# Order, engines and filler products listed anew, from the first loads to the first late expert, in a kernel of attention and four experts

## The chip, the cores and the metric

The kernel runs on one core of a Trainium2 chip. The metric is device time in microseconds (us) for one execution, lower being better. Before the change it is 454.83 us, the median of three runs (452.33 to 455.21).

A core has engines with a queue of instructions each: PE (TensorE, matrix products), DVE (VectorE), ACT (ScalarE), POOL (GpSimd), and SP, which here only issues loads and stores. They wait for each other by semaphores. Every engine takes its own instructions strictly in the order in which they were written.

## The reference

```python
def _attn_ref(q, k, v):                      # B, H, S, D = 2, 8, 576, 64
    q_d, k_d, v_d = (mean over groups of 4 positions of q, k, v)
    out_d  = softmax(q_d @ k_d.T / 8) @ v_d  # 144 x 144 for each head
    out_up = np.repeat(out_d, 4, axis=2)
    mask = np.abs(pos[:, None] - pos[None, :]) < 4
    out_local = softmax(where(mask, q @ k.T / 8, -1e9)) @ v
    return out_up + out_local

def _moe_ref(x, domain_probs, w1, w2):       # x 1152 x 512, 4 experts, w1 512 x 1024, w2 1024 x 512
    p = domain_probs / (domain_probs.sum(-1, keepdims=True) + 1e-09)
    for e in range(4):
        out += p[:, e:e + 1] * (np.maximum(x @ w1[e], 0.0) @ w2[e])
    return out
```

The tokens x of the second function are the output of the first, 2 batches by 576 positions, 8 heads by 64 side by side. All inputs and the output are float32.

## The kernel before

**Stages.** Attention is done in four parts, `a0` to `a3`: two batches by two halves of 288 positions. Expert 0 runs between them in blocks of tokens `m00` to `m03` (256, 256, 256 and 384 tokens), as soon as the parts that make those tokens are through. The late experts 1 to 3 follow, each as sums of tokens and weights (`x1` to `x4`, `s`, `t`, `w`) and products `p110`, `p510` and so on (L1033), then second products `s110` ... (L1222, L1235). Before them `a0` alone has only small work for PE.

**Steps of an attention part**, by the last part of their names, with the line that issues them:

- loads (SP): `q0n`, `k00n`, `k01n`, `v00n`, `v01n` in halves of four heads (L244); `a1q.0` to `.3` and `k10r`, `k11r` by rows (L255); `vw` windows of v (L276); `raw100` ... `raw201` weights of expert 0 (L290); `praw` the probabilities.
- rows: `q0r`, `k00r`, `k01r` copy the loaded heads into another order (L189 on ScalarE, L191 on VectorE). `k00t`, `qt` are transposes on PE (L340), four to a step, `k00te`, `qte` the copies back (L183 to L191).
- pooled path, 144 columns: `qds`, `k00ds` and `k01ds` sum rows (L375, L376), `qdt`, `k00dt`, `k01dt` transpose them (L381), `qde`, `k00de` copy them; in later parts `qd` and `k10d` reduce instead (L359). `ds` products (L675), `dm` maximum (L689), `de` exponential (L697), `da`, `db` sum and reciprocal (L707, L709), `dq` share (L714), `dt` transpose (L722), `dc` copy, `dv` product with the summed values `v00d`, `v01d` (L745), `xd` copy. These come in four groups, 0 to 3; of `ds` and `dv` two groups go in one piece, with the later of the two names.
- local path, three tiles of 96 positions, 0 to 2: `sc0.0` and `sc0.1` are the products of a tile's scores for four heads each (L522), in `a0` with two products that add the mask (L512); `madd` (L545), `max` (L556, L560), `sub` (L567, L571), `exp` (L574), `sum`, `eps`, `rec` (L578 to L586), `norm` (L589), `blk` (32x32 transposes on VectorE, L593), `pv` product with the window (L602).
- `xs` adds both paths (L615), `xh` is its rounded copy and `xl` the remainder (L626).

**Steps of expert 0.** `whi` is a weight's rounded copy (L189 on ScalarE) and `wlo` its remainder (L306, 128x1024; POOL does it in four pieces, VectorE in one). `m00.m0` to `.m7` are the first products of block m00, 12 matmuls each (L778), `r` and `l` their rectified high and low parts (L785 and L789), `m00.o00` ... the second products in four parts to a tile of 128 tokens (L803), `g` the weighted result (L810).

**What sets the order.** Nothing is planned when the program is built. Every piece of work is a named step with a default engine; a table `ENGINE` overrides the engine of some (V, G or A), and a table `ORDER` lists all 1320 names:

```python
def step(name, eng, deps, fn):
    steps[name] = (ENGINE.get(name, eng), deps, fn)
...
for name in order(steps):          # order() returns ORDER
    steps[name][2]()
```

So each engine's queue holds its steps in the order of the table. A step that must wait holds up everything behind it on the same engine. A third table, `WARM`, gives 46 counts: step `warm7` puts `WARM[7]` products of a 64x64 tile of zeros on PE, whose result nobody reads.

```python
for _ in range(n):
    nc.tensor.matmul(T["wps"][:64, :64], wz, wz, start=True, stop=True)
```

**Buffers that tie steps.** Small products share a pool of three PSUM tiles and the larger ones another pool of three (`ps_g`, `ps_m`). The rows of `a2q` go where those of `k11r` were, so its load waits for the four transposes `k11t`; `a1q` goes where `q0r` was.

Of the kernel before, what the change touches and what calls it, by code (L numbers as in the profile page):

```python
# [1381 lines left out]
```

## Time and profile before

| | us |
|---|---|
| median of three runs | 454.83 (452.33 to 455.21) |
| the profiled execution, its own time | 456.84 |
| its span | 455.1 |

| engine | busy in the span | instructions |
|---|---|---|
| PE, products | 443.3 us (97%) | 4266 |
| PE, weight loads | 420.6 us (92%) | 4266 |
| DVE | 337.8 us (74%) | 592 |
| ACT | 208.3 us (46%) | 391 |
| POOL | 104.7 us (23%) | 126 |

The profile is one execution. The span goes from its first to its last instruction; the profiled execution's time is 1.7 us longer. The mean granted clock of PE over the span is 0.977 of full speed. TensorE's clock has two levels, 1.2 and 2.4 GHz; a granted clock of 0.50 is the lower and 1.00 the upper. A float32 product appears as two records on PE, so six 64x64 products are a group of x12.

In a chain of waits a row says from when on, and how long, an engine or a DMA held up the work that ended last. A row of the view of lines gives minimum, median and maximum duration in ns. Where a row of a timeline ends in brackets, they hold the engine's idle time just before it and what ended that.

### The profile page before, as it was taken

To read this page: it belongs to the slowest core of one execution; us is meant where nothing else is said; L and a number is where in the kernel's file an instruction comes from. 1 tells how busy PE (TensorE), PEld (TensorE's weight loads), DVE (VectorE), ACT (ScalarE), POOL (GpSimd) and SP (SyncE) were. 2 spreads that over 40 slices of the span, in tenths; PEclk is the share of its full clock that TensorE was granted. 3 is DMA by queue.
4 is the path that set the end of the run, shared out by engine and by line. 5 is a ranking of instruction groups with operands and counts; after the bars stand their busy time and mean duration, and the time that the engine had idled before them with its cause. 6 is when DMAs were issued, how large, how long until landed. Compare 5 with 4: busy or idle time off the path is not lost.

```text
span 455.1 us, 10197 instructions
## 1 busy us (share of the span) xinstructions
PE 443.3 (97%) x4266; PEld 420.6 (92%) x4266; DVE 337.8 (74%) x592; ACT 208.3 (46%) x391; POOL 104.7 (23%) x126
## 2 busy tenths in 40 slices
PE   8998798999999999999999999999999999999996
PEld 7777687898897998999999999999999999999996
DVE  4669778678678898556579985666799846678983
ACT  4666542332141433554466517444664164446630
POOL 5559941140011000121332121012321100013020
PEclk9758999999999999999999999999999999999999
DMA  7889424501101030662466494334655923135135
GB/s 172 218 196 241 102 58 108 105 18 34 37 1 48 2 93 1 169 109 81 83 118 91 112 168 94 46 101 88 104 80 130 185 58 46 48 62 94 31 94 163
DMA packets 69086, 43.11 MB, mean 95 GB/s; under 512 B 27632, under 2 KB 66992, under 8 KB 69040
## 3 DMA queue, kind: packets, MB, share of 16 engines
q1 hardware_dynamic: 55392, 30.14, 25.4%
q0 software_dynamic: 13648, 12.32, 18.4%
q8 instruction: 33, 0.54, 0.5%
q14 instruction: 13, 0.11, 0.1%
HBM read 36.69 MB, written 2.36 MB: 86 GB/s over the span
## 4 chain that ended last, share of the span: by engine, by line
PE 87%; POOL 4%; DMA 4%; DVE 2%; SPq 1%; issue 1%; ACT 1%; POOLq 0%; ACTq 0%
PE ps L1033 29%; PE ps L1222 26%; PE ps L1235 4%; PE m03h L778 4%; PE m03o L803 4%; POOL wlo L306 3%; PE m02h L778 3%; PE m01h L778 3%; PE m01o L803 3%; PE m02o L803 2%; PE m00o L803 2%; PE m00h L778 1%; DMA acc<-in_q_dram 1%; DMA vw<-in_v_dram 1%; DMA q0n<-in_q_dram 1%; SPq L276 1%
## 5 line engine op out<-in xcount | busy, mean ns | idle before, releaser
L1222 PE MATMUL ps<-slot,unit 128*128 128x256 f32 x1008 | 119.7, 280 | 0.0
L1222 PEld LDWEIGHTS ps<-slot,unit 128*128 128x128 f32 x1008 | 119.0, 189 | 0.0
L1033 PE MATMUL ps<-xhi,slot 128*128 128x288 f32 x384 | 66.5, 295 | 0.0
L1033 PE MATMUL ps<-xc,slot 128*128 128x288 f32 x432 | 59.8, 295 | 0.0
L1033 PEld LDWEIGHTS ps<-xc,slot 128*128 128x128 f32 x432 | 58.2, 188 | 0.0
L1033 PEld LDWEIGHTS ps<-xhi,slot 128*128 128x128 f32 x384 | 56.3, 188 | 0.1
L1045 ACT ACTIVATE H<-ps 128x288 f32<-128x288 f32 x72 | 27.8, 411 | 50.1 <-PE ps L1033 50.0
L1082 POOL DMA_DIRECT2D raw<-in_moe_w_dram x15 | 19.5, 1297 | 133.4 <-DVE slot L1088 74.7
L987 DVE TENSOR_TENSOR slot<-raw,slot 128x1792 fp32r<-128x1792 f32 x12 | 24.3, 2022 | 26.7 <-PE ps L1033 24.3
L1049 DVE TENSOR_TENSOR H<-H,ps 128x288 f32<-128x288 f32 x72 | 29.3, 449 | 19.6 <-PE ps L1033 19.6
L189 ACT CAST slot<-raw 128x1024 fp32r<-128x1024 f32 (+1 forms) x33 | 41.8, 1279 | 2.8 <-DVE raw L981 2.0
L1033 PE MATMUL ps<-xlo,slot 128*128 128x288 f32 x192 | 41.1, 295 | 0.0
L1133 ACT ACTIVATE unit<-H 128x512 fp32r<-128x512 f32 (+1 forms) x24 | 20.0, 844 | 28.6 <-DVE H L1049 18.2
L1137 ACT ACTIVATE unit<-H 128x1024 fp32r<-128x1024 f32 x18 | 19.1, 1062 | 29.1 <-PE ps L1222 19.2
L1033 PEld LDWEIGHTS ps<-xlo,slot 128*128 128x128 f32 x192 | 30.7, 188 | 0.0
L1120 DVE SCALAR_TENSOR_TENSOR H<-H 128x1024 f32<-128x1024 f32 (+1 forms) x18 | 28.1, 1574 | 1.9 <-ACT H L1047 1.6
L1146 DVE SCALAR_TENSOR_TENSOR unit<-H,unit 128x1024 fp32r<-128x1024 f32 x18 | 22.0, 1222 | 8.1 <-ACT unit L1137 8.0
L1088 DVE TENSOR_TENSOR slot<-raw,slot 128x1024 fp32r<-128x1024 f32 x21 | 25.3, 1218 | 2.4 <-ACT slot L189 2.4
L1142 DVE SCALAR_TENSOR_TENSOR unit<-H,unit 128x512 fp32r<-128x512 f32 (+1 forms) x24 | 22.5, 954 | 3.0 <-ACT unit L1133 3.0
L1244 DVE SCALAR_TENSOR_TENSOR acc<-ps,npr,acc 128x256 f32<-128x256 f32 x48 | 20.7, 476 | 2.9 <-PE ps L1222 2.9
L306 POOL TENSOR_TENSOR wlo<-raw,whi 128x256 fp32r<-128x256 f32 x28 | 21.7, 805 | 1.2 <-ACT whi L189 1.1
L975 POOL DMA_DIRECT2D raw<-in_moe_w_dram x8 | 11.8, 1469 | 41.0 <-DMA raw<-in_moe_w_dram 23.2
(328 smaller groups left out, 775.8 us busy)
## 6 DMA issues: line engine op xcount, KB each, us to landing
raw<-in_moe_w_dram POOLq DMA_DIRECT2D x15, 512.0 KB, 6.1
raw<-in_moe_w_dram SPq DMA_DIRECT2D x24, 256.0 KB
raw<-in_moe_w_dram SPq DMA_DIRECT2D x12, 512.0 KB
...
```

What stands on the lines that cost most here:

```text
L189: nc.scalar.copy(out_, in_)
L306: eng.tensor_tensor(a[:, us], b[:, us], c[:, us], ALU.subtract)
L778: nc.tensor.matmul(ps[:, :n], w[:, d, cc:cc + P], x[:, d, n0:n0 + n], start=i == 0, stop=i == len(terms) - 1,)
L803: nc.tensor.matmul(ps[:, cs], T[f"{nm}t{f}"][:, hpart, cc:cc + P], w[:, f % 4, cs], start=f == 0 and x == 0, stop=f == KF - 1 and x == 2,)
L987: engine(f"wo{e}{i}").tensor_tensor(w1tile(i, 1), raw1(e, i), f32(w1tile(i, 0)), ALU.subtract)
L1033: nc.tensor.matmul(bank(acc_, n, i)[:, :NH // 2], w[:, d * P:(d + 1) * P], x[:, d, n * (NH // 2):(n + 1) * (NH // 2)], start=u == 0 and fi ...
L1045: nc.scalar.mul(dst, at, -1.0)
L1049: nc.vector.tensor_tensor(dst, dst, at, ALU.add)
L1088: engine(f"bo{e}{m}").tensor_tensor(w2tile(m, 1), raw2(q), f32(w2tile(m, 0)), ALU.subtract)
L1120: nc.vector.scalar_tensor_tensor(at[o], at[x], 0.0, at[y], ALU.max, op)
L1142: nc.vector.scalar_tensor_tensor(o, x, 0.0, y, ALU.max, ALU.subtract)
L1222: nc.tensor.matmul(ps[:, t * 256:t * 256 + 256], a[:, f, t * P:t * P + P], b[:, f], start=first_ and (t, f, x) == (0, 0, 0), stop=(t, f, x ...
```

## The change

Only the three tables are written anew. No function changes, no step is added or removed, and the numbers computed are the same.

`WARM` goes from 69 products to 86. Steps that carry none or few may now stand elsewhere, too.

```diff
-WARM = [14, 0, 0, 0, 0, 0, 0, 0, 0, 0, 0, 0, 0, 1, 0, 0, 1, 0, 0, 0, 0, 3, 0, 0, 0, 0, 1, 3, 2, 0, 0, 0, 0, 0, 2, 0, 1, 3, 0, 0, 14, 6, 6, 3, 3, 6]
+WARM = [12, 0, 0, 0, 2, 0, 0, 3, 2, 0, 2, 0, 2, 1, 0, 0, 2, 0, 0, 0, 0, 6, 0, 0, 0, 0, 0, 2, 0, 3, 1, 0, 0, 0, 2, 0, 0, 3, 2, 0, 14, 6, 6, 3, 9, 3]
```

`ENGINE` differs in 43 entries. To VectorE go `q0r.0`, `k00te.0`, `k01r.1`, `a0.dc2`, `a0.xh0`, `a1.dc1`, `a1.dc2`, `a1.xh0`, `k11te.0`, `k11te.3`, `whi201.1`, `a2.qte.0`, `a3.qte.0`, `a3.xh2` from ScalarE and `v01d.1`, `v10d.1`, `a1.norm0`, `a1.sub2`, `a1.dq0`, `a2.xl0`, `a3.xl2` from POOL. To POOL go `k00ds.1`, `k01ds.0`, `v11d.0`, `a0.norm2`, `a1.norm1`, `a2.norm0`, `a2.sub0`, `a2.dq2`, `a2.xl1`, `a3.norm1`, `a3.sub0`, `a3.dq0`, `a3.dq2` and to ScalarE `k10te.3`, `a1.xh1`, `a2.dc0`, all from VectorE. A few more entries repeat a default or name a load, and move nothing.

`ORDER` differs up to about the first expert's second products; from `s110` on PE has the rows it had. The loads on SP stand in another order: before, `k01n`, `v00n`, `v01n.1`, `raw100`, `v01n.0`, the four of `a1q`, `vw01`, `raw101`; after, `v01n.0` ahead of `k01n`, then `v00n.0`, `v01n.1`, `vw01`, `a1q.1`, `v00n.1`, `a1q.2`, `raw100`, `a1q.0`, `vw00`, `a1q.3`, `raw101`, `raw200`. Two lines of it, around the first scores:

```diff
-    k00te.1 k00te.0 a0.qte.0 warm4 k00t.2 warm19 a0.qte.2 a0.qte.1 k00t.3 k00te.3 k00te.2 a0.qte.3 a0.sc0.0 a0.sc0.1
+    a0.qte.0 k00te.1 v00d.1 k00t.2 warm19 vw00 a0.qte.3 a1q.3 a0.qte.1 a0.qte.2 a0.sc0.0 k00te.2 warm5 k00t.3 warm4
```

In the rows that follow, the names behind a line number are result and operands, with the number of the buffer; `wps` is the unread result of the warm products.

PE before, from the transposes of the pooled q (`a_qdt`) to the first tile's scores (`a0sl` from keys `kT` and queries `a0qT`):

```order
L381 MATMUL a_qdt<-ident,a0.qdp 128x72 x4
L232 MATMUL wps<-wz 64x64 x6
L340 MATMUL k00t_184<-ident,acc 128x72 x4
L340 MATMUL k00t_189<-ident,acc 128x72 x4
L232 MATMUL wps<-wz 64x64 x6
...
L232 MATMUL wps<-wz 64x64
L340 MATMUL k00t_279<-ident,acc 128x72 x4
L340 MATMUL k00t_286<-ident,acc 128x72 x4
L512 MATMUL a0sl<-mask,ident 128x128 x2
L522 MATMUL a0sl<-kT_121,a0qT 32x32 x32
L381 MATMUL k00dt<-ident,k00dp 128x72 x4
```

PE now, at the same place:

```order
L381 MATMUL a_qdt<-ident,a0.qdp 128x72 x4
L232 MATMUL wps<-wz 64x64 x9
L340 MATMUL k00t_185<-ident,acc 128x72 x4
L232 MATMUL wps<-wz 64x64 x2
...
L340 MATMUL k00t_284<-ident,acc 128x72 x4
L512 MATMUL a0sl<-mask,ident 128x128 x2
L522 MATMUL a0sl<-kT_240,a0qT 32x32 x16
L340 MATMUL k00t_319<-ident,acc 128x72 x4
L232 MATMUL wps<-wz 64x64 x3
L381 MATMUL k01dt<-ident,k01dp 128x72 x4
L232 MATMUL wps<-wz 64x64 x2
L522 MATMUL a0sl<-kT_240,a0qT 32x32 x16
```

The scores of the first tile were one row of 32 and are now two of 16; the last key transposes, warm products and `k01dt` stand between them, and more warm products stand ahead.

PE before, behind the first group of value products `a0po` and ahead of `a0.pv0` (`a0pv`):

```order
L722 MATMUL a0pdt_568<-ident,a0pd_507 72x72 x4
L722 MATMUL a0pdt_578<-ident,a0pd_529 72x72 x4
L232 MATMUL wps<-wz 64x64 x3
L602 MATMUL a0pv_588<-ptb_92,vw_334 64x96 x8
L745 MATMUL a0po<-a0pts_573,vd_265 64x72
```

PE now:

```order
L722 MATMUL a0pdt_576<-ident,a0pd_523 72x72 x4
L722 MATMUL a0pdt_590<-ident,a0pd_537 72x72 x4
L232 MATMUL wps<-wz 64x64 x11
L602 MATMUL a0pv_608<-ptb_92,vw_289 64x96 x8
L745 MATMUL a0po<-a0pts_584,vd_268 64x72
```

Eleven warm products stand there instead of three.

VectorE before, in part a1, from the remainder `wlo200.1` (L306) to two of m00's low parts (L789):

```order
L306 TENSOR_TENSOR wlo_815<-raw_650,whi_693 128x1024
L789 SCALAR_TENSOR_TENSOR m00t_843<-m00h_773,m00t_843 128x256
...
L191 COPY a1pts_899<-a1pdt_891 72x288
L707 TENSOR_SCALAR a1dsm<-a1dsm 72x2
L560 TENSOR_REDUCE a1mx_927<-a1pm_846 128x8
L789 SCALAR_TENSOR_TENSOR m00t_854<-m00h_792,m00t_854 128x256
L689 TENSOR_REDUCE a1dmx<-a1sd_834 72x2
```

VectorE now:

```order
L306 TENSOR_TENSOR wlo_834<-raw_617,whi_709 128x1024
...
L191 CAST whi_827<-raw_672 128x1024
L714 TENSOR_TENSOR a1pd_829<-a1pd_829,a1dsm 72x288
...
L191 COPY a1pts_914<-a1pdt_906 72x288
L560 TENSOR_REDUCE a1mx_919<-a1pm_832 128x8
L789 SCALAR_TENSOR_TENSOR m00t_889<-m00h_809,m00t_889 128x256
L560 TENSOR_REDUCE a1mx_944<-a1pm_882 128x8
L707 TENSOR_SCALAR a1dsm<-a1dsm 72x2
```

The step `m00.l3` (the second L789 before, `m00t_889` now) stood behind `a1.da2` (L707) and now stands ahead of it. The cast `whi201.1` and the share `a1.dq0` (L714) have come in ahead of the copy `a1.dc0` (`a1pts`).

## Rows read from the trace of the kernel before

**Rows 1.** The page: busy time and instructions by engine; the chain's shares by engine.

```profile
PE 443.3 (97%) x4266; PEld 420.6 (92%) x4266; DVE 337.8 (74%) x592; ACT 208.3 (46%) x391; POOL 104.7 (23%) x126
...
PE 87%; POOL 4%; DMA 4%; DVE 2%; SPq 1%; issue 1%; ACT 1%; POOLq 0%; ACTq 0%
```

**Rows 2.** Stretches: start:end, length, busy by engine (instructions), PEclk, DMA share, GB/s.

```profile
9.60:16.50 6.90, 6.18 (x102) 5.17 (x104) 6.24 (x15) 4.81 (x9) 1.47 (x3) 1.00 0.96 234
16.50:37.00 20.50, 20.23 (x297) 16.71 (x298) 12.72 (x46) 11.68 (x32) 14.46 (x20) 0.50 0.85 215
37.00:43.00 6.00, 5.26 (x186) 4.55 (x187) 5.61 (x12) 3.94 (x7) 5.98 (x9) 1.00 1.03 266
43.00:79.50 36.50, 32.26 (x372) 27.69 (x359) 29.18 (x72) 16.61 (x44) 19.16 (x30) 1.00 0.42 90
79.50:182.20 102.70, 102.52 (x1103) 90.16 (x1104) 84.35 (x173) 34.19 (x84) 12.85 (x17) 1.00 0.16 38
```

**Rows 3.** The chain that ended last: start, length, engine, result, line.

```profile
79.50 0.95 PE a_qt L340 x12
...
182.28 44.57 PE ps L1033 x336
```

**Rows 4.** Waits of PE from 0 to 190 us: total, times, longest.

```profile
PE m00h L778 <- DVE m00t L789: 1.3, 1, 1.3
...
PE a1pdt L722 <- POOL a1pd L714: 1.2, 1, 1.2
...
PE a_qt L340 <- DMA acc<-in_q_dram: 0.3, 1, 0.3
```

**Rows 5.** Timeline of PE, 9.5 to 44 us: start, length, operation.

```profile
9.53 0.91 PE L232 MATMUL wps<-wz 128*64 128x64 f32 x12
...
15.59 0.36 PE L522 MATMUL a0sl<-kT,a0qT 64*32 64x32 f32 x32
...
16.99 0.36 PE L522 MATMUL a0sl<-kT,a0qT 64*32 64x32 f32 x16 [0.15 <-ACT a0qT L183]
...
22.38 1.59 PE L675 MATMUL a0sd<-kd,a0qd 64*72 64x144 f32 x8
...
28.77 1.33 PE L232 MATMUL wps<-wz 128*64 128x64 f32 x10
30.03 0.70 PE L722 MATMUL a0pdt<-ident,a0pd 72*72 72x72 f32 x4
...
35.69 1.31 PE L745 MATMUL a0po<-a0pts,vd 72*64 72x72 f32 x16
```

**Rows 6.** Timeline of PE behind 45 us, the same kind of product as at 22.38.

```profile
45.59 0.71 PE L675 MATMUL a1sd<-kd,a1qd 64*72 64x144 f32 x8
```

**Rows 7.** Timeline of VectorE, 37 to 46 us.

```profile
37.48 0.56 DVE L615 TENSOR_TENSOR a0x<-a0pv,a0xd 128x384 f32<-128x384 f32 x1 [0.21 <-ACT a0xd L189]
37.96 1.77 DVE L593 STREAM_TRANSPOSE ptb<-a0pm 32x256 f32<-32x256 f32 x4
...
42.24 0.41 DVE L191 CAST xhi<-a0x 128x384 fp32r<-128x384 f32 x1
...
44.24 0.54 DVE L626 TENSOR_TENSOR xlo<-a0x,xhi 128x384 fp32r<-128x384 f32 x1
44.71 0.74 DVE L359 TENSOR_REDUCE a1qd<-a1qT 128x144 f32<-128x576 f32 x1
```

**Rows 8.** Durations of single lines: ns minimum/median/maximum, first and last start.

```profile
L714 DVE TENSOR_TENSOR a1pd<-a1pd,a1dsm x1: 445/445/445, 57.7 to 57.7; 72x288 f32<-72x288 f32 x1
...
L707 DVE TENSOR_SCALAR a0dsm<-a0dsm x4: 165/166/475, 25.4 to 31.7; 72x2 f32<-72x2 f32 x4
L707 DVE TENSOR_SCALAR a1dsm<-a1dsm x4: 456/592/1360, 47.7 to 56.7; 72x2 f32<-72x2 f32 x4
...
L189 ACT CAST whi<-raw x8: 1035/1042/1051, 31.8 to 49.5; 128x1024 fp32r<-128x1024 f32 x8
...
L189 ACT COPY kT<-k01t x3: 673/673/710, 22.0 to 26.7; 128x288 f32<-128x288 f32 x3
```

More of the change, by code (lines that the diff above doesn't have):

```diff
@@ L31 @@
-    a0.sum0 a0.db1 a0.ds2 a0.ds3 a0.dm2 a0.dm3 k01te.3 warm9 a0.sc2.1 warm35 warm38 a0.dq0 a0.dt0 a0.dc0 a0.eps0
-    a0.dq1 a0.rec0 a0.max2 a0.de2 a0.sub2 warm28 warm27 a0.dt1 a0.norm0 a0.da2 a0.dc1 a0.db2 a0.dq2 a0.de3 a0.da3
-    a0.eps1 a0.db3 a0.blk0.1 a0.rec1 a0.exp2 a0.blk0.0 a0.sum2 a0.dq3 a0.norm1 whi100.1 wlo100.1 a0.eps2 a0.blk1.1
-    a0.rec2 a0.blk1.0 warm26 a0.dv1 a0.dv0 a0.dt2 a0.dc2 a0.norm2 whi101.0 a0.dt3 a0.dv2 warm8 a0.dc3 warm44 a0.pv0
-    a0.dv3 a1.qt.1 whi100.0 a0.xd a0.xs0 a1.qt.3 warm45 a0.pv1 a1.qt.2 a0.blk2.0 a0.blk2.1 vw02 k10r.3 raw200 k10r.2
@@ new lines @@
+    a0.rec0 a0.dc0 a0.de2 warm28 a0.sub2 warm27 a0.dt1 a0.da2 a0.de3 a0.db2 a0.dc1 a0.dq2 a0.exp2 a0.da3 a0.eps1
+    a0.norm0 a0.rec1 a0.db3 a0.blk0.1 a0.dq3 a0.sum2 a0.blk0.0 a0.norm1 whi100.1 a0.eps2 warm1 wlo100.1 a0.rec2 a0.dv1
+    warm26 a0.dv0 a0.dt2 a0.norm2 whi101.0 a0.dc2 a0.blk1.1 a0.blk1.0 a0.dt3 warm8 a0.dc3 warm44 a0.dv2 a0.pv0 raw200
+    a0.dv3 a1.qt.1 whi100.0 a0.xd a1.qt.3 warm45 a0.pv1 a1.qt.2 a0.blk2.0 a0.xs0 a0.blk2.1 vw02 k10r.3 k10r.2 praw
+    raw201 k10r.1 a0.xh0 a0.xs1 wlo100.0 a1.start a0.xl0 a1.qte.1 a1.qte.3 wlo101.0 a1.qte.2 a0.pv2 a1.qt.0 a0.xs2
@@ new lines @@
+    whi200.1 a0.xh2 whi101.1 wlo101.1 whi200.0 a1.qte.0 a0.xh1 a0.xl2 a0.xl1 a1.qd.0 warm32 a1.sc1.1 a1.sc2.1 a1.sc2.0
+    a1.sc0.1 a1.qd.1 m00.m0 a1.ds1 a1.ds0 m00.m3 a1.dm0 m00.r0 whi201.0 a1.de0 a1.madd2 wlo200.1 a1.dm1 m00.l0 a1.da0
+    a1.sc1.0 wlo200.0 a1.sc0.0 a1.ds2 a1.db0 a1.madd0 a1.dm2 whi201.1 a1.de1 m00.r3 a1.dq0 a1.da1 m00.m2 a1.dt0 a1.db1
+    a1.madd1 a1.dc0 a1.de2 a1.max2 m00.l3 a1.ds3 a1.dq1 kstart1 m00.m1 m00.r2 m00.r1 a1.max0 a1.da2 m00.l1 a1.db2
+    a1.dm3 a1.sub0 a1.dq2 a1.sub2 a1.exp0 a1.dt1 m00.m6 a1.de3 a1.dc1 k10r.0 m00.m4 wlo201.1 k11r.3 vw03 k11r.0 k11r.1
@@ new lines @@
+    k11r.2 vw04 v10n.1 vw05 v11n.1 m00.l2 m00.r4 a1.da3 a1.dv1 a1.dv0 a1.db3 a1.exp2 a1.dq3 a1.dt2 k10t.2 m00.o00
+    a1.dt3 a1.dc2 a1.max1 m00.r6 a1.dc3 a1.sum0 m00.l4 wlo201.0 a1.sum2 m00.m5 k10t.1 a1.dv3 k10t.0 gate a1.sub1
+    a1.eps0 m00.o01 a1.dv2 m00.m7 a1.eps2 a1.rec0 a1.norm0 m00.l6 k10te.2 a1.blk0.0 a1.rec2 a1.norm2 a1.exp1 m00.r5
+    a1.sum1 m00.l5 a1.eps1 k10te.0 a1.xd a1.blk0.1 k11t.1 a1.pv0 k10te.1 k11te.1 a1.rec1 m00.r7 a1.norm1 a1.xs0
+    a1.blk2.1 a1.blk2.0 k11t.0 k11t.3 k10t.3 m00.o02 k11t.2 m00.o10 k10te.3 a1.blk1.0 a1.xh0 a1.blk1.1 a1.pv2 m00.l7
```

88 lines of the change are left out of this document (39 added, 49 removed).

## The prediction, made before the change was run

> **What bounds the kernel now.** The page's busy shares and its chain come first: PE is busy 97% of the span and holds 87% of the chain that ended last [rows 1]. That share is a mean over stages, so the second view is busy time by stretch [rows 2]. From 79.5 us on PE is never free: 102.5 of 102.7 us up to 182.2, and from there the late experts' products follow each other without a pause [rows 2, 3]. Nothing the change does behind 79.5 us can bring the end forward; it can only open gaps. What counts is when PE reaches the transposes `a2.qt` that start at 79.50 [rows 3].
>
> Ahead of that the kernel waits in three ways. From 16.5 to 37 us the granted clock is 0.50, the lower of TensorE's two levels, and PE is busy 20.23 of 20.50 us: there PE is the bound, at half speed [rows 2]. From 37 to 43 VectorE is busy 5.61 of 6.00 us and PE follows it. From 43 to 79.5 PE does expert 0's first products among attention a1's small ones; it has the full clock and stands idle about 4.2 us [rows 2]. The two longest waits, 1.3 and 1.2 us, end on VectorE's `m00.l3` and on POOL's `a1.dq0`, which stands behind `wlo200.0` on POOL; one for the a2q load is 0.3 [rows 4].
>
> **Part 1, up to the first scores.** What fills PE between `a0.qdt` and the scores grows from 15 to 21 warm matmuls, at 0.15 us each (12 records, two to a matmul, in 0.91 us [rows 5]). `k00te.0` moves to VectorE, `q0r.0` too, and `k00ds.1` leaves it. `v01n.0` is now loaded ahead of k01n: one load of 72x4x256 floats is 0.29 MB, 1.3 us at 234 GB/s [rows 2], so VectorE's `k01ds.1` starts that much later, and `k01r.0` and `a0.max0` stand behind it; VectorE has room for that, busy 12.72 of the 20.50 us from 16.5 on [rows 2], so I cost it at nothing, and at 1.3 us if it turns out to be on the path. The second half of the scores also waits for `k00t.3`, which now follows the first half. I put the first half's end at 16.65 us instead of 15.95.
>
> **Part 2, the clock.** Before, the clock fell at about 16.5 us, after 7 us in which PE did transposes with 15 warm matmuls and the first masks and scores between them [rows 2, 5]. It was back at 37.0, after `a0.pv0` and `a0.dv3` had run nearly without a transpose. After the change there are 21 warm matmuls ahead of the scores, five more right behind the first half, and the masks stand closer to the end of the same stretch. No row shows whether that is enough. So both cases are priced.
>
> If the clock stays up past the scores: before, PE ran from 16.99 to 23.97 (the end of `a0.ds1`) without a pause, 7.0 us at the lower level. To this the change adds a transpose step (0.7, as the four of `a0.dt1`) and five warm matmuls (5 x 0.27 from 10 records in 1.33 us [rows 5]), 9.0 us; at the upper level half, since the pair of `ds` products takes 0.71 us there against 1.59 [rows 5, 6]. From 16.65 that ends at 21.2; ScalarE's copy `k01te.1` (about 0.7) then ends last, and I take 22.1: 1.9 us earlier. From there to the end of `a0.dt1` (30.73) PE's own 2.7 us (0.70 + 1.33 + 0.70, two transposes of a kind and the warm matmuls between [rows 5]) halve, and the warm matmuls between go from five to four: 1.2 us less. `a0.dt1` ends at 27.6, 3.1 us earlier.
>
> Behind `a0.dt1` only `a0.dv0` stands between it and the second group of warm matmuls, so I expect the clock to fall there, some 12 us later than before. Then the eleven warm matmuls that replace four cost 7 x 0.27 = 1.9 us, and `a0.dv0` waits 0.7 for VectorE's copy: the sum `a0.xs0` starts 9.4 us behind `a0.dt1` instead of 6.75, at 37.0 against 37.48 [rows 7]. **Term: -0.5 us** (-1.4 if the clock does not fall there).
>
> If the clock falls as before: the stretch is PE's own, and it gets 14 more warm matmuls (26 against 12 between the scores' second half and `a0.pv0`) at 0.27, 3.8 us, and `k00t.3` at 0.5. **Term: +4.3 us.**
>
> **Part 3, VectorE from 37.5 to 45.** From `a0.xs0` to the end of `a0.xl1` VectorE took 37.48 to 44.78, 7.3 us [rows 7]. After: `a0.blk2.0` (half of the four blocks' 1.77) stands ahead of `a0.xs0`, `a1.qd.1` (0.74) behind `a0.xl1`; `a0.xh0` comes from ScalarE (0.41 as the cast of the same size). 7.3 - 0.9 - 0.7 + 0.4 = 6.1. Against it `a0.norm2` moves from VectorE to POOL, between two `wlo100` steps, and `a0.blk2.0` can wait for it. I take 6.6. **Term: -0.7 us** (bounds 0 and -1.2).
>
> **Part 4, 43 to 79.5 us.** `m00.l3` now stands ahead of `a1.da2`, behind which it waited; so of PE's 1.3 us I take 0.8 as gone (`whi201.1`, below, pushes what is behind it); the 0.3 us for the a2q load goes too, since `k11t.2`, which frees its place, comes earlier by as much. `a1.dq0` moves from POOL to VectorE, where it takes 0.45 [rows 8], but `whi201.1`, a cast of 1024 columns, now stands ahead of it there: 1.04 us on ScalarE, 1.1 on VectorE by the cast of 384 in 0.41 [rows 7, 8]. So the 1.2 us wait of `a1.dt0` stays. `a1.ds1` gains one of 0.5, since it needs `a1.qd.1`; the wait for `k10te.3` becomes one for `k11te.0` of about the same length. In all -0.8 - 0.3 + 0.5. **Term: -0.6 us.** Bounds: VectorE gets 3.6 us more work here (`whi201.1` 1.1, four copies and shares at 0.45, `a1.xh0` 0.41, two key copies at 0.68 as on ScalarE [rows 8], less 1.1 given away) against 7.3 us of idle; if all lies on the path, it is -1.6 for the two waits and 3.6 of work, +2.0; if none does, -1.6.
>
> One row speaks against moving such work to VectorE: the scaling `L707` of 72x2 takes 0.17 us in a0 and 0.59 in the median, up to 1.36, in a1, while POOL does its `wlo` pieces [rows 8]. The Trainium skill, "SBUF — State Buffer", section "Who interferes with whom", says that a VectorE cast or tensor_scalar in its two-port mode and a GpSimd instruction shut each other out for the whole of one instruction. By that rule `whi201.1` would also wait for one `wlo` piece, and the sum would be 0.7 us worse; the trace agrees with it in the rows of L707.
>
> **Part 5, behind 79.5 us.** The reordering of a2, a3, expert 0's other blocks and the first late products costs nothing as long as PE has work queued, which it had for 102.5 of 102.7 us. VectorE is busy 84.35 us of these with 173 instructions, half a microsecond each [rows 2]; I bound what one late step could cost by three of them, +1.5, and take 0. `ws11` and `x3.l` stand later, but so does their first reader. The entries for `k10r.3`, `k11r.1` and `wlo201.0` change no instruction.
>
> **Sum.** -0.5 - 0.7 - 0.6 = -1.8 us. The profiled execution took 456.84 us, so 455.0 for one like it; the median of the runs shown is 2.0 us under that, 454.83, and **453.0 us** is the forecast against it.
>
> **Rivals.**
> (a) The clock falls at 16.5 us as before: +4.3 - 0.7 - 0.6 = +3.0, **457.8**. For it: the transposes still make up most of the stretch. It decides from the first lower-level record before 20 us on. If the clock then comes back only after m00's first products have begun, it is 2 us worse.
> (b) The clock holds up to `a0.pv0` too: -1.4, and `a0.pv0` and `a0.dv3` (1.31 at the lower level) save 1.0 more: -3.7 in all, **451.1**. Against it: the thin stretch around `a0.dv0`.
> (c) VectorE becomes the bound between 43 and 79.5 us: -0.5 - 0.7 + 2.0 = +0.8, **455.6**. For it: it was busy 29.2 of 36.5 us before and gets 3.6 us more [rows 2]. Against: that still leaves 3.7 us free.
> (d) It changes nothing that can be seen, since from 79.5 us on PE is full: ruled out as a reason, because whatever is won or lost ahead of 79.5 us is passed on whole.
>
> **Chances.** The forecast 0.48, (a) 0.30, (b) 0.12, (c) 0.10. Own range of the forecast: 450.5 to 455.5. Range for 8 in 10: from under (b) to over (a), 449.5 to 459.0. A measurement of this kernel can tell about 1%, 4.5 us, from no change. Faster by more, under 450.3: 0.08 of (b) and 0.09 of the forecast, 0.17. Slower by more, over 459.4: 0.12 of (a) and 0.03 of (c), 0.15. Between: 0.68.
>
> **What would show it.** The clock by microsecond from 14 to 40 us decides between forecast, (a) and (b); `a0.dt1` should end near 27.6 us and `a0.xl1` near 43.6. The wait of m00.m6 for `m00.l3` should be gone, that of `a1.dt0` still there, now on VectorE. `a2.qt` should start near 77.7, and PE have no wait of over 0.3 us behind it. Wrong it is if PE waits behind 79.5 us, or if `a0.xs0` starts more than 2 us off 37.0.

## The result, and the profile after

The change makes the kernel slower by 0.6%: 458.67 us median (455.92 to 460.85) against 456.27 (452.33 to 459.83), 20 runs each. The ratio is 1.0063, 95% interval 1.0039 to 1.0086, so 2.9 us with an interval of 1.8 to 3.9. Forecast were 453.0 us and a range of 449.5 to 459.0. The median lies inside that range, beside rival (a)'s 457.8, and on the other side of no change than the forecast. The forecast was set against 454.83 us, the median of three runs; as changes, -1.8 us was forecast, and 2.4 (medians) to 2.9 (ratio) measured. The profiled execution took 458.57 us.

The page after, as [rows 1]:

```profile
PE 445.2 (97%) x4300; PEld 422.5 (92%) x4300; DVE 343.6 (75%) x598; ACT 202.9 (44%) x380; POOL 110.9 (24%) x131
...
PE 89%; DVE 6%; DMA 3%; SPq 1%; issue 1%; ACT 0%; DVEq 0%; ACTq 0%
```

The same stretches as [rows 2]:

```profile
9.60:16.50 6.90, 6.70 (x106) 5.60 (x105) 4.43 (x8) 4.08 (x8) 6.67 (x9) 1.00 0.89 188
16.50:37.00 20.50, 18.05 (x290) 14.64 (x288) 15.66 (x44) 10.78 (x30) 12.67 (x18) 0.65 1.02 244
37.00:43.00 6.00, 5.34 (x60) 4.82 (x60) 5.45 (x13) 1.67 (x3) 5.64 (x10) 0.50 0.74 226
43.00:79.50 36.50, 33.74 (x498) 29.21 (x495) 30.72 (x76) 16.18 (x41) 19.05 (x27) 0.95 0.35 76
79.50:182.20 102.70, 102.59 (x1111) 90.38 (x1110) 83.11 (x174) 33.76 (x84) 16.80 (x22) 1.00 0.20 46
```

PE is free 2.45 us between 16.5 and 37, where before it was free 0.27, and the lower level of the clock now covers 37 to 43. The waits of PE up to 190 us, as [rows 4], and its timeline, as [rows 5]:

```profile
PE k01t L340 <- DVE kr L191: 2.2, 1, 2.2
PE a1pdt L722 <- DVE a1dsm L707: 1.2, 1, 1.2
...
PE a1pv L602 <- ACT m00t L785: 0.8, 1, 0.8
PE a0pv L602 <- DVE a0pts L191: 0.7, 1, 0.7
...
PE a1pv L602 <- DVE kT L191: 0.6, 1, 0.6
```

```profile
19.33 0.35 PE L522 MATMUL a0sb<-kT,a0qT 64*32 64x32 f32 x32
21.89 0.69 PE L340 MATMUL k01t<-ident,kr 72*128 72x72 f32 x8 [2.20 <-DVE kr L191]
...
22.91 1.42 PE L675 MATMUL a0sd<-kd,a0qd 64*72 64x144 f32 x8
...
31.01 0.70 PE L722 MATMUL a0pdt<-ident,a0pd 72*72 72x72 f32 x4
...
34.86 2.61 PE L232 MATMUL wps<-wz 128*64 128x64 f32 x22
38.13 1.55 PE L602 MATMUL a0pv<-ptb,vw 128*64 128x96 f32 x16 [0.66 <-DVE a0pts L191]
```

The scores at 19.33 still have the upper level (0.35 us for 32 records). Then PE pauses 2.2 us. The clock falls at 22.5, behind that pause, and is back at 46.4. `a0.dt1` ends at 31.7 us (30.7 before, 27.6 forecast), `a0.pv0` starts 3.8 us later than before, `m00.m0` 5.0 later, `p110` 1.5 later (183.66 against 182.12).

VectorE ahead of that pause, and around `a0.eps2`, an instruction of 128x8 values (L582); after it POOL in the same microseconds:

```profile
13.94 1.09 DVE L375 TENSOR_TENSOR k01dt<-k01n 72x512 f32<-72x512 f32 x1 [2.30 <-DMA k01n<-in_k_dram]
...
15.83 1.76 DVE L191 COPY kr<-k01n 72x1024 f32<-72x1024 f32 x1
...
19.66 0.62 DVE L453 TENSOR_TENSOR v01n<-v01n 72x512 f32<-72x512 f32 x1
20.31 0.82 DVE L454 TENSOR_TENSOR vd<-v01n 72x256 f32<-72x256 f32 x1
21.06 0.68 DVE L191 COPY kr<-k01n 72x1024 f32<-72x1024 f32 x1
...
35.54 1.98 DVE L582 TENSOR_SCALAR a0sm<-a0sm 128x8 f32<-128x8 f32 x1
...
37.68 0.40 DVE L191 COPY a0pts<-a0pdt 72x288 f32<-72x288 f32 x1
```

```profile
34.72 2.78 POOL L306 TENSOR_TENSOR wlo<-raw,whi 128x256 fp32r<-128x256 f32 x4
```

`k01r.0` (21.06) stands behind a load, behind `k01r.1` (15.83), the memsets and `v01d.1` (19.66 to 21.14, which was POOL's). `a0.eps2` takes 1.98 us and ends as POOL ends `wlo100.1` (37.50); `a0.dc2` (37.68) is behind it, and `a0.pv0` needs the PSUM tile that `a0.dc2` frees.

**A fact about the measurement.** Each execution's records give its span and mean granted clock, so twice the missing clock times the span is its time at the lower level. It differs from one execution to the next: 0 to 36 us over 150 executions of before that ran beside the experiments, 20 in the mean, and 15 to 32, 24.7 in the mean, over the 20 of after. Over before's executions each microsecond at the lower level goes with 0.19 us of time. Among executions with a clock of 0.980 to 0.986 the median is 455.9 us before (35 of them) and 457.2 after (4); with 0.968 to 0.974 it is 458.0 (52) and 458.8 (11). So some 1 us of the loss is there at equal clock, and some 0.9 (4.7 us at 0.19) goes with the longer lower level. Where it helps below, "at equal clock" is the difference between the mean of a kernel's executions and of before's beside them, with 0.19 us taken off for each microsecond at the lower level; it is an estimate, worked out from these records.

### The profile page after: what moved, and what is told of

Read it like the earlier page. It is cut to its first block, busy times and chain, and to the rows that moved or that the text cites. A ratio compares the mean times of both kernels' runs of the same rounds, so it can differ in the third digit from the quotient of the medians.

```text
span 456.8 us, 10277 instructions
## 1 busy us (share of the span) xinstructions
PE 445.2 (97%) x4300; PEld 422.5 (92%) x4300; DVE 343.6 (75%) x598; ACT 202.9 (44%) x380; POOL 110.9 (24%) x131
## 4 chain that ended last, share of the span: by engine, by line
PE 89%; DVE 6%; DMA 3%; SPq 1%; issue 1%; ACT 0%; DVEq 0%; ACTq 0%
PE ps L1033 29%; PE ps L1222 26%; PE ps L1235 4%; PE m03h L778 4%; PE m03o L803 4%; PE m01h L778 3%; PE m02o L803 3%; PE m01o L803 3%; PE m02h L778 2%; DMA k01n<-in_k_dram 2%; PE m00o L803 2%; PE m00h L778 2%; DVE ptb L593 1%; PE a_qt L340 1%; PE a0pv L602 1%; DMA vw<-in_v_dram 1%
## 5 line engine op out<-in xcount | busy, mean ns | idle before, releaser
L1082 POOL DMA_DIRECT2D raw<-in_moe_w_dram x15 | 19.5, 1297 | 156.6 <-DVE slot L1088 88.1
L1033 PEld LDWEIGHTS ps<-xlo,slot 128*128 128x128 f32 x192 | 30.7, 188 | 0.0
L1142 DVE SCALAR_TENSOR_TENSOR unit<-H,unit 128x512 fp32r<-128x512 f32 (+1 forms) x24 | 22.5, 954 | 4.1 <-ACT unit L1133 4.1
L306 POOL TENSOR_TENSOR wlo<-raw,whi 128x256 fp32r<-128x256 f32 x28 | 22.1, 821 | 4.2 <-ACT whi L189 4.1
L1235 PE MATMUL ps<-slot,slot 128*128 128x256 f32 x144 | 18.1, 283 | 0.0
```

The costliest lines, as they stand in the source:

```text
L1033: nc.tensor.matmul(bank(acc_, n, i)[:, :NH // 2], w[:, d * P:(d + 1) * P], x[:, d, n * (NH // 2):(n + 1) * (NH // 2)], start=u == 0 and fi ...
L1142: nc.vector.scalar_tensor_tensor(o, x, 0.0, y, ALU.max, ALU.subtract)
L1235: nc.tensor.matmul(w, a[:, 2 * f + r], b[:, f], start=(c, r, f, x) == (1, 1, 0, 0), stop=(r, f, x) == (0, 3, 2), skip_group_check=True,)
```

## The experiments

All ratios are to the kernel before, with the 95% interval; 0.001 is 0.46 us. A difference between the ratios of two kernels is uncertain by both intervals, 1.6 to 2.4 us. Edits are to the tables only.

### Which part loses: fronts and backs exchanged

The tables are joined at one name; the entries of `ENGINE` and `WARM` go with their names. e4 has the front of before:

```diff
+n = BEFORE.index("a0.xd") + 1
+ORDER = BEFORE[:n] + [x for x in AFTER if x not in BEFORE[:n]]
```

> The three tables of before up to a0.xd (about 37.4 us in the profile before) and those of after for every step behind it. Theory A, the whole loss lies in the front, and the part behind it is faster by about what the trace of after wins between a1.sc2.0 and p110 (3.4 us), some of it only slack given back: the median is 1 to 3 us under that of before, and p110 starts at 179.5 to 181 with the front as in before. Theory B, what after wins behind 47 us is only slack that a late front uses up: the median is that of before within 0.5 us. Theory C, the part behind costs something of its own: over before by 0.5 us or more.

Measured: 452.62 us, 0.9934 (0.9902 to 0.9965), 3.0 us faster than before. Theory A. The whole loss lies ahead of `a0.xd`.

e8 is the counterpart, `AFTER[:n]` and then the names of before:

> The three tables of after up to a0.xd, and those of before for every step behind it: the counterpart of the kernel with the front of before. If front and back add, the front alone costs what lies between after and that kernel, 6 us by the medians, and this kernel takes 460.5 to 463 us, 4 to 6 over before. If the waits that before has behind a0.xd (1.3 us of m00.m6 for m00.l3, 1.2 of a1.dt0, VectorE's chain up to a0.xl1) use up part of a late front, it is 2 to 3.5 us over before.

Measured: 461.55 us, 1.0084 (1.0056 to 1.0112), 3.8 us slower than before. The front costs 3.8 us with the back of before and 5.9 with its own (1.0063 against 0.9934). The 3.8 lie between the two theories' ranges, and the two costs differ by no more than the intervals, so the time decides neither. At equal clock the back of after gains 3.1 us with the front of before (e4) and 2.9 with the front of after (after against e8), which speaks for parts that add.

e5 takes only the last part from after, `n = BEFORE.index("m00.o12") + 1`:

> The three tables of before for every step up to m00.o12 (PE is there at 79.2 us in the profile before) and those of after for every step behind it. From the start of a2.qt to the start of p110 PE is never free in either profile, yet the steps of that stretch occupy PE 106.7 us in before and 104.7 in after. Theory P, neighbours on PE decide how long a step takes: the pooled products a2.ds0 and a2.ds1, each 0.64 us where another step stands between them, take 0.65 together where they follow each other, and so do a3.ds1 and a3.ds2; the median is 1.3 to 2.1 us under that of before. Rival, no gap means no gain, and the 2 us are a difference between two executions: the median is that of before within 0.5 us.

Measured: 455.63 us, 0.9975 (0.9944 to 1.0006), 1.1 us faster, a little under the 1.3 to 2.1 expected and with an interval that just takes in no change; at equal clock 1.4 us (1.0 to 1.9). The trace shows the same. Chain of e5, then of after, first transposes of a2 and start of the late experts:

```profile
78.80 0.51 PE a_qt L340 x8
...
179.86 5.17 PE ps L1033 x39
```

```profile
82.77 0.51 PE a_qt L340 x8
...
183.83 1.19 PE ps L1033 x9
```

That is 101.06 us in both, against 102.78 in [rows 3], in stretches in which PE is never free. e4 against e5 leaves 1.9 us for the middle, from `a0.xd` to `m00.o12`, give or take 2.0; at equal clock 1.6, give or take 0.6.

Most of why PE takes less for the same steps stands in the timelines of PE, before and then after:

```profile
83.53 0.71 PE L675 MATMUL a2sd<-kd,a2qd 64*72 64x144 f32 x4
...
86.45 0.71 PE L675 MATMUL a2sd<-kd,a2qd 64*72 64x144 f32 x4
```

```profile
88.81 0.72 PE L675 MATMUL a2sd<-kd,a2qd 64*72 64x144 f32 x8
...
123.00 0.72 PE L675 MATMUL a3sd<-kd,a3qd 64*72 64x144 f32 x8
```

`a2.ds0` and `a2.ds1` read different halves of the rows (64 of 128 each). Apart they take 0.71 us each, next to each other 0.72 together, and so do `a3.ds1` and `a3.ds2`. The next step starts 0.64 us behind a single one and 0.65 behind a pair, so the two pairs are some 1.2 of the 1.7 us; the rest was not traced. That it is the different halves which count is argued: no run puts two steps of the same half side by side. e6 does only the pairing to the kernel before, for a2 and a3:

```diff
-a2.qd.1 a2.ds0 m00.o13 a2.sc0.1 a2.sc0.0 m00.g1 m01.l0 a2.ds1
+a2.qd.1 m00.o13 a2.sc0.1 a2.sc0.0 m00.g1 m01.l0 a2.ds0 a2.ds1
...
-a3.madd1 a3.ds1 m02.m1 m02.m5 a3.ds2
+a3.madd1 m02.m1 m02.m5 a3.ds1 a3.ds2
```

> The kernel before, with two steps moved in the table: a2.ds0 to just ahead of a2.ds1 (some 2.5 us later), and a3.ds1 to just ahead of a3.ds2, so that the products of an even and an odd group, which read different halves of the rows, follow each other on PE. Theory P: the four steps lose 0.3 us each, 1.2 us in all, and the median is 0.8 to 1.3 us under that of before. Rival: PE's time there does not depend on the neighbour; the median is that of before within 0.4 us, or over it where VectorE now waits for the later maximum.

Measured: 457.83 us, 1.0024 (0.9993 to 1.0056), no gain; at equal clock 1.1 us slower (0.7 to 1.4). In its timeline the a2 pair is 0.72 us in one, as expected, and what stands behind it comes 0.75 us sooner after `a2.qt`. The a3 pair did not come together, as its second half waits:

```profile
PE a3sd L675 <- DVE a2x L615: 1.1, 1, 1.1
```

```profile
122.10 0.68 PE L675 MATMUL a3sd<-kd,a3qd 64*72 64x144 f32 x4 [1.10 <-DVE a2x L615]
...
123.79 1.22 PE L778 MATMUL m02h<-xhi,wlo 128*128 128x256 f32 x4
```

Behind that wait the granted clock is 0.50 from 122.9 to 126.3 us: the product at 123.79 takes 1.22 us, where its like takes 0.73 in the profile before. From `a2.qt` to the late experts this trace has 104.45 us instead of 102.78, so the wait and the clock behind it cost more than the a2 pair gains. The pair's time is shown, and that it can be had by moving two names alone is not: the vector work around them has to move too, as in after.

### What in the front loses

e1 moves one copy on VectorE in the kernel after:

```diff
-k01ds.1 k01ds.0 k01r.1 clear v00d.0 raw100 a0.start warm24 v01d.1
+k01ds.1 k01ds.0 k01r.0 k01r.1 clear v00d.0 raw100 a0.start warm24 v01d.1
...
-a0.sc1.0 k01r.0 a0.max0
+a0.sc1.0 a0.max0
```

> The kernel after, with k01r.0 (the copy of the first key rows of half 1) one step earlier on VectorE, ahead of k01r.1, the memsets and v01d.1; max0 and sub0 stay where they are. In the profile after, PE pauses 2.2 us ahead of k01t.1, from 19.7 to 21.9, and the clock falls at 22.7. Theory 1, the pause is what brings the lower level: PE goes on at 19.7, the clock stays at the upper level up to at least 26 us, a0.dt1 ends at 28 to 29 (after: 31.7), and the median lies 1.5 to 3 us under that of after, about where the kernel before is or under it. Theory 2, the clock falls here whatever is done, since from k01t on transposes make up most of PE's work: the pause goes, the clock falls between 20 and 23 all the same, a0.dt1 ends at 29.5 to 30.5, and the median is 0 to 1 us under that of after.

Measured: 457.41 us, 0.9996 (0.9969 to 1.0022), 3.0 us under after by the ratios. PE's timeline:

```profile
19.30 0.72 PE L340 MATMUL k01t<-ident,kr 72*128 72x72 f32 x8
...
22.88 1.02 PE L512 MATMUL a0sl<-mask,ident 128*128 128x128 f32 x4 [1.22 <-DVE a0pm L567]
```

The pause is gone from `k01t.1`, and the time is theory 1's. But half of it turns up ahead of the third tile's scores, which wait for `a0.sub0`, still behind `v01d.1`; the clock falls there, at 23.1, and `a0.dt1` ends at 30.7, as theory 2 had it. e2 tells these apart, by filling the pause:

```diff
-a0.sc1.0 k01r.0 a0.max0 k01t.1 a0.sub0 k01t.0 a0.sc1.1 warm17
+a0.sc1.0 k01r.0 a0.max0 warm17 k01t.1 a0.sub0 k01t.0 a0.sc1.1
...
-WARM[17] = 0
+WARM[17] = 14
```

> The kernel after, with 14 warm products (2.1 us at 0.15) put into the pause of PE ahead of k01t.1, and nothing moved. Theory 1, it is the pause that brings the lower level: the clock stays up to at least 26 us although k01t.1 still starts at about 21.9; a0.dt1 ends at about 29.7, 2 us ahead of after, and the median is 1 to 2 us under that of after. Theory 2, the clock falls whatever is done: it falls between 22 and 24 as in after, a0.dt1 ends at 31.5 to 32, and the median is that of after within 0.5 us.

Measured: 457.84 us, 1.0029 (1.0003 to 1.0056), 1.6 us under after, just within the intervals. The filled pause and the stretches of its profile:

```profile
19.71 1.84 PE L232 MATMUL wps<-wz 128*64 128x64 f32 x28
22.15 0.69 PE L340 MATMUL k01t<-ident,kr 72*128 72x72 f32 x8 [0.60 <-DVE kr L191]
```

```profile
16.50:22.50 6.00, 5.40 (x124) 4.70 (x123) 5.64 (x9) 1.18 (x3) 4.79 (x5) 1.00 0.86 188
22.50:30.00 7.50, 6.44 (x153) 4.84 (x151) 5.78 (x24) 5.20 (x19) 3.85 (x6) 1.00 0.79 164
30.00:38.00 8.00, 6.94 (x68) 6.17 (x70) 7.48 (x19) 4.19 (x9) 7.15 (x12) 0.54 1.03 309
```

With the pause filled and nothing else changed the clock stays up to 30.6 us, and `a0.dt1` ends at 29.5. Theory 1: here the pause brings the lower level. Mean time at it falls from 24.7 to 18.1 us. Not every pause does so: those of 1.3 and 1.2 us in [rows 4] lie in a stretch at 1.00 [rows 2].

e11 asks for the load's share:

```diff
-k00n.0 k00n.1 warm37 q0r.0 k00r.0 v01n.0 warm36
+k00n.0 k00n.1 warm37 q0r.0 k00r.0 warm36
...
-k01n.0 k01n.1 v00n.0 v01n.1
+k01n.0 k01n.1 v00n.0 v01n.0 v01n.1
```

> The kernel after with one load moved: v01n.0 again behind k01n and v00n.0, ahead of v01n.1. The prediction costed the load ahead of k01n at nothing, and at 1.3 us if it turned out to be on the path. Theory 1, it is on the path with the rest: VectorE's k01ds.1, which waits 2.3 us for k01n in after, starts 1.2 to 2.3 us earlier, k01r.0 ends 1.2 to 2 us earlier, and PE's pause of 2.2 us falls to under 1; the median is 0.7 to 2 us under that of after. Theory 2, the work put ahead of k01r.0 on VectorE alone makes the pause (v01d.1 1.5 us, k01r.1 1.8): v01d.1 now waits for its load instead, k01r.0 ends within 0.5 us of where it did, and the median is that of after.

Measured: 458.62 us, 1.0022 (0.9991 to 1.0053), between the two theories by the ratio and at after's time by the median. The profiled execution had the lower clock from 15.7 us on, so the pause can't be read in it. VectorE's rows can:

```profile
13.65 1.25 DVE L375 TENSOR_TENSOR k01dt<-k01n 72x512 f32<-72x512 f32 x1
...
20.94 1.75 DVE L191 COPY kr<-k01n 72x1024 f32<-72x1024 f32 x1
```

`k01ds.1` no longer waits for its load, but VectorE gets to it only 0.3 us earlier than in after (13.94), and `k01r.0` ends later, at 22.7 us. So the first step of theory 1 did not come in this execution; the load's share of the time stays open.

e3 moves one step on POOL in the kernel after:

```diff
-wlo100.1 a0.rec2 a0.dv1 warm26 a0.dv0 a0.dt2 a0.norm2
+a0.rec2 a0.dv1 warm26 a0.dv0 a0.dt2 a0.norm2 wlo100.1
```

> The kernel after, with one remainder of POOL, wlo100.1, behind a0.norm2 instead of ahead of it. In the profile after, a0.eps2, a 128x8 instruction of VectorE, takes 1.99 us (35.54 to 37.52) and ends as POOL ends the last piece of wlo100.1 (37.49). Theory 1, the two engines shut each other out: a0.eps2 takes under 0.25 us, a0.dc2 ends at about 36.3 instead of 38.1, a0.blk2.0 1.5 us earlier; PE, which has eleven warm products up to 37.5, starts a0.pv0 at 37.5 instead of 38.1, and the median is 0.5 to 1 us under that of after. Rival, a0.eps2 waits for its operand and not for POOL: its 2 us stay, and the median is that of after.

Measured: 456.46 us, 1.0001 (0.9975 to 1.0026), 2.8 us under after, well over the 0.5 to 1 expected. VectorE's timeline:

```profile
35.90 0.17 DVE L582 TENSOR_SCALAR a0sm<-a0sm 128x8 f32<-128x8 f32 x1
...
36.22 0.40 DVE L191 COPY a0pts<-a0pdt 72x288 f32<-72x288 f32 x1
```

The 1.8 us are gone with POOL's work: theory 1. What I had not expected is that the clock comes back at 38 us instead of 46 in its profile; the mean time at the lower level is 17.1 us against 24.7.

e9 gives after three fillers ahead of `a0.pv0`:

```diff
-WARM[8], WARM[44] = 2, 9
+WARM[8], WARM[44] = 0, 3
```

> The kernel after with three warm products ahead of a0.pv0, as before has, instead of eleven. The prediction charged the eleven with 1.9 us. Theory 1, they stand in a wait: a0.pv0 needs a tile that a0.dc2 frees, and VectorE gets to a0.dc2 behind the 2 us of a0.eps2; PE waits 2.5 to 3 us ahead of a0.pv0 instead of 0.7, a0.pv0 starts within 0.5 us of where it did, and the median is that of after within 0.7 us, or over it if the pause keeps the clock down longer. Theory 2, they are pure cost: a0.pv0 starts 1.9 us earlier, and the median is 1 to 2 us under that of after.

Measured: 459.06 us, 1.0050 (1.0021 to 1.0078), after's time. The wait took the fillers' place:

```profile
PE a0pv L602 <- DVE a0pts L191: 2.4, 1, 2.4
```

e7 mends all of this: e1's and e3's moves, e9's fillers, and `a0.dc2` on ScalarE ahead of `whi101.0`:

```diff
-ENGINE["a0.dc2"] = "V"
+ENGINE["a0.dc2"] = "A"
```

> The kernel after with four things mended in its front: k01r.0 ahead of k01r.1 on VectorE; wlo100.1 behind a0.norm2 on POOL; a0.dc2 back on ScalarE, ahead of whi101.0; three warm products ahead of a0.pv0 instead of eleven. Theory 1, each removes a wait of its own on the way to a0.pv0, and they add: no pause ahead of k01t.1, a0.eps2 under 0.25 us, a0.pv0 at 35.3 to 36.5, a0.xs0 at 37.5 to 38.5, and the median is 4 to 6 us under that of after, 452.5 to 454.5. Rival, the time follows how long the clock is low and not these waits: the median is that of the kernels with one of them, 2 to 3 us under that of after.

Measured: 454.88 us, 0.9955 (0.9927 to 0.9983), 4.9 us under after and 1.0 over e4, a difference within the intervals. `a0.xs0` starts at 37.8 us, as expected, and `a0.pv0` at 34.7, sooner than that. Single moves of 3.0 and 2.8 us come to 4.9 with the two other edits: these two places are most of the front's loss. What `a0.dc2` on ScalarE and the three fillers add was not run by itself.

### The middle

e10 moves the one step on which the prediction put most of its term, in the kernel before:

```diff
-a1.da2 a1.ds3 kstart1 a1.dq1 m00.m1 m00.r2 m00.r1 a1.max0 m00.l3
+m00.l3 a1.da2 a1.ds3 kstart1 a1.dq1 m00.m1 m00.r2 m00.r1 a1.max0
```

> The kernel before with one step moved on VectorE: m00.l3 ahead of a1.da2 instead of behind it and a1.max0. The prediction put 0.8 us on it. If the wait of 1.3 us of m00.m6 is PE's own, it goes or falls to under 0.3, what follows on PE comes 0.8 to 1.3 us earlier, and the median is 0.5 to 1.3 us under that of before. Rival, the next wait takes it up (k10te.3 or the a2q load at the end of the stretch, 0.9 and 0.3 before): a2.qt starts within 0.4 us of where it did, and the median is that of before.

Measured: 457.77 us, 1.0018 (0.9983 to 1.0054). The wait of `m00.m6` falls from 1.3 to 0.2 us, and from the end of `a1.dt0` to `a2.qt.0` the trace has 25.9 us instead of 27.4 (0.3 of it is the wait for the a2q load). The time as it stands does not show it: this kernel's executions happened to have 26 us at the lower level in the mean, those of before beside them 18, though the step stands behind it all. At equal clock the kernel is 0.7 us faster (0.2 to 1.2), within the 0.5 to 1.3 expected; by the ratio alone a gain of 1 us can't be told.

e12 has the front of before, and `whi201.1` moved:

```diff
-whi201.1 a1.de1 m00.r3 a1.dq0 a1.da1 m00.m2 a1.dt0 a1.db1 a1.madd1 a1.dc0
+a1.de1 m00.r3 a1.dq0 a1.da1 m00.m2 a1.dt0 a1.db1 a1.madd1 a1.dc0 whi201.1
```

> The front of before up to a0.xd, the tables of after behind it, and one more step moved: the cast whi201.1 on VectorE behind a1.dc0 instead of ahead of a1.dq0. In the kernel with the front of before PE waits 1.2 us for a1.dt0. If the cast is what a1.dq0 is behind, that wait falls by 0.6 to 0.8 us and the median lies 0.3 to 0.8 us under that kernel's, 3 to 4.5 under before. Rival, a1.dq0 waits for VectorE's small scalings while POOL does wlo200.0: the wait stays over 0.9 us, and the median is that of the kernel with the front of before.

Measured: 454.40 us, 0.9925 (0.9897 to 0.9954). The wait of `a1.dt0` falls from 1.2 to 0.5 us; 0.4 us against e4 is within the intervals.

### Fillers and the clock

Left was whether the mended front is slower than before's because its lower level lies later. e13 puts eleven fillers ahead of `a0.pv0` back into e7. e14 takes the added ones around the first scores out of e7, e16 out of after (the first pair of lines), and e15 adds such to e4 (the second):

```diff
-WARM[29], WARM[10], WARM[16], WARM[4], WARM[30], WARM[12] = 3, 2, 2, 2, 1, 2
+WARM[29], WARM[10], WARM[16], WARM[4], WARM[30], WARM[12] = 0, 0, 1, 0, 0, 0
...
-WARM[41], WARM[10], WARM[16], WARM[12] = 6, 0, 1, 0
+WARM[41], WARM[10], WARM[16], WARM[12] = 9, 2, 2, 5
```

> The kernel with four things mended, with eleven warm products ahead of a0.pv0 again instead of three. Theory C, they help the clock back to its upper level (in the kernel with wlo100.1 moved, which had them, the mean time at the lower level was 17 us and the clock back at 38): the clock is back at 37 to 39 us in the profile instead of 46, a0.pv0 starts at 35.8 to 36.8, 1.5 us later than with three, a1.sc2.0 no later, and the median lies between 1 us under and 0.5 over that of the mended kernel. Rival, they only cost: the clock comes back where it did, and the median is 1 to 2 us over.

> The kernel with four things mended, with eleven of the warm products around the first scores taken away, so that 15 stand between a0.qdt and the scores, as in before, and none between the two halves. Theory L, it matters where the lower level lies: the clock falls at 15 to 18 us again and is back at 36 to 39; a0.pv0 comes up to 1.5 us later than in the mended kernel, a1.sc2.0 1 to 2 us earlier (42.2 to 43.2 instead of 44.2), and the median is 1 to 2 us under that of the mended kernel, at 452.9 to 454. Theory N, only the length of the lower level matters, or the fillers are what kept it short: the clock falls early and the median is the mended kernel's or up to 2 us over it.

> The kernel with the front of before, with eleven more warm products around the first scores: three, two and one ahead of them as in after, five behind them. Theory L: the clock stays up past the first scores, falls at 20 to 27 us and is back only at 42 to 47; the median is 1 to 2.5 us over that of the kernel with the front of before (ratio to before 0.996 to 1.000 instead of 0.993). Theory N: a0.dt1 comes 1 to 2 us earlier and that is passed on; the median is that of the kernel with the front of before or up to 1 us under it.

> The kernel after, with the same eleven warm products around the first scores taken away, and nothing mended. This is rival (a) of the prediction made on purpose: the clock falls at 15 to 18 us. Rival (a) priced it at 3.8 us of fillers at the lower level, of which eight ahead of a0.pv0 remain. Theory L: the pause ahead of k01t.1 shrinks to under 1 us, since PE is at the lower level when it comes there, the clock is back by 40 us, and the median is 0.5 to 2 us under that of after. Theory N: the median is that of after or up to 2 us over it.

| | median us | ratio (interval) | mean us at the lower level |
|---|---|---|---|
| e7, mended | 454.88 | 0.9955 (0.9927 to 0.9983) | 17.7 |
| e13, eleven ahead of `a0.pv0` | 453.68 | 0.9947 (0.9924 to 0.9970) | 11.5 |
| e14, eleven fewer early | 455.53 | 0.9956 (0.9932 to 0.9980) | 21.4 |
| e4, front of before | 452.62 | 0.9934 (0.9902 to 0.9965) | 19.0 |
| e15, eleven more early | 454.47 | 0.9949 (0.9915 to 0.9984) | 17.6 |
| after | 458.67 | 1.0063 (1.0039 to 1.0086) | 24.7 |
| e16, eleven fewer early | 460.15 | 1.0075 (1.0046 to 1.0104) | 33.5 |

Theory L finds no support, and only e16 tests it: there the lower level lies early (14.4 to 38.4 us in its profile), and it is not faster. In e14's profile it lies at 25.9 to 46.4 us and in e15's from before 12 to 41.6, not where the theory wanted it; their times are those of e7 and e4 within the intervals. The lower level is shorter with the fillers, by 9 us in after and 6 in e13 (the 4 in e7 are within the scatter), and the time hardly follows. e13's clock is back at 37.9 us, where theory C has it; profile of e13:

```profile
30.00:38.00 8.00, 7.74 (x76) 6.62 (x76) 5.63 (x18) 5.03 (x13) 5.20 (x9) 0.50 1.00 224
38.00:46.00 8.00, 7.22 (x209) 6.18 (x205) 7.70 (x14) 5.64 (x8) 7.98 (x11) 1.00 0.65 183
```

e17 is e13 with e12's move, e18 is e12 with eleven fillers:

```diff
-WARM[8], WARM[44] = 0, 3
+WARM[8], WARM[44] = 2, 9
```

> The mended kernel with eleven fillers ahead of a0.pv0, and the cast whi201.1 on VectorE behind a1.dc0 instead of ahead of a1.dq0. If that step's 0.5 to 0.7 us are PE's own here too: the wait of a1.dt0 is under 0.7 us and the median 0.3 to 0.8 us under that of the mended kernel with eleven (ratio to before 0.992 to 0.994 instead of 0.9947). Rival, VectorE's later work is delayed by the cast and PE waits elsewhere: the ratio stays at 0.994 to 0.996.

> The kernel of e12 (front of before, the rest of after, whi201.1 moved) with eleven warm products ahead of a0.pv0 instead of three. Theory C, they bring the clock back early in this front too: mean time at the lower level 10 to 16 us instead of 19 to 23, few executions over 25, the median 0.5 to 2 us under that of e12 in the same terms (ratio 0.988 to 0.992). Rival, they cost 8 x 0.27 = 2.2 us at the lower level where PE is already the bound: a0.pv0 starts 2 us later, the clock comes back where it did, and the ratio is 0.994 to 0.998.

e17: 454.97 us, 0.9945 (0.9916 to 0.9974). The wait of `a1.dt0` is 0.5 us instead of e13's 1.2, but the time is no better than e13's. e18: 452.25 us, 0.9893 (0.9850 to 0.9936), six executions, 12.8 us at the lower level in the mean (3.6 to 27.2), and in its profile the clock is up between 30.2 and 33.6 us:

```profile
30.00:33.00 3.00, 2.12 (x28) 1.46 (x26) 2.12 (x8) 2.40 (x9) 1.30 (x2) 0.96 1.05 320
33.00:37.00 4.00, 3.92 (x44) 3.82 (x45) 3.77 (x12) 2.22 (x4) 3.60 (x7) 0.58 1.12 163
```

That is the fastest version by its median: the front of before with eleven fillers ahead of `a0.pv0`, and the rest of after with `whi201.1` moved, 4.9 us faster than before (2.9 to 6.8) and 7.8 faster than after. What the fillers add to e12, 1.5 us, is within the intervals.

## Why the prediction was wrong, step by step

**Part 1 failed.** It had the later load ahead of `k01r.0`, and set the cost at nothing because VectorE was busy only 12.7 of 20.5 us [rows 2]. A share says nothing about what stands ahead of one step. The last key sum did end 1.3 us later (15.9 against 14.6), what it had priced for the load, but VectorE got `k01r.1` and `v01d.1` in front of `k01r.0` as well (1.76 and 1.48 us), which the prediction left out. The step ended 4.5 us later than before, and PE waited 2.2 us. e1 puts 3.0 us on the order of these steps.

**Part 2 was right where it was least sure, and wrong in its sum.** The clock stayed up past the first scores. It then fell at 22.5 us instead of behind `a0.dt1`, because of that pause (e2), and was back at 46.4. `a0.xs0` started at 41.1 us, 4 off the 37.0 forecast, which the prediction named as a sign of being wrong. The front, forecast at -0.5 us with both parts, costs 3.8 to 5.9 (e8, and after against e4). A slip in the sum is small beside that: 2.7 us halved, with a filler fewer, is 1.5 us less and not 1.2. Its 1.9 us for eleven fillers was no cost: they stood in a wait for `a0.dc2` (e9). That wait was the second failed step: `a0.dc2` had been moved to VectorE behind `a0.eps2`, and `a0.eps2` is held up while POOL does `wlo100.1` (e3, 2.8 us). I had the rows of L707 for such a thing [rows 8], and applied them only to `whi201.1`. With both waits gone e7 is 2.1 us faster than before (0.8 to 3.3), close to the forecast's 1.8, but not by its way: in e7's profile the clock is down from 22.9 to 46.7 us.

The Trainium skill, "SBUF — State Buffer", section "Who interferes with whom", has VectorE's tensor_scalar, in its two-port mode, and a GpSimd instruction exclude each other for a whole instruction. The trace of after agrees as to the exclusion (1.98 us beside POOL's pieces, 0.17 without), but it lasted for the three pieces that were left, not for one; in the profile before the same instruction took 0.18 us beside such pieces.

**Parts 3 and 4 held, as far as can be told.** Forecast were -1.3 us together; e4 against e5 gives -1.9, give or take 2.0, and at equal clock -1.6, give or take 0.6. From `a0.xs0` to the end of `a0.xl1` it is 6.6 us in e4's profile and 6.4 in e18's, against 7.3 before and 6.6 forecast. `m00.m6`'s wait is gone and `a1.dt0`'s is 1.2 us on VectorE, as forecast. `whi201.1` took 0.68 us, not 1.1; `a1.dq0` took 0.98, not 0.45, beside POOL's `wlo200.0`. Rival (c) is out, as this stretch gains time.

**Part 5 was wrong in principle.** "Nothing the change does behind 79.5 us can bring the end forward" took a full PE for one whose time is fixed. The late order saves 1.7 us in the trace (1.1 by e5's ratio, 1.4 at equal clock).

The Trainium skill, "TensorE: Matmul & The Clock Gate", section "Part 3: Packing small matmuls — row/col tiling", says that small products in different groups of rows run at the same time. The `ds` rows agree, 0.72 us for two steps against 0.71 for one.

**Rival (a)** came within 0.9 us (as a change, +3.0 against 2.9) by luck: its fall at 16.5 us did not come, and what cost the time were waits that it does not have. e16, where the clock does fall early, takes 1.0075, after's time; but it has eleven fillers fewer, so it does not test rival (a)'s price.
